# Sliding-window attention with sinks and a token-and-channel mixer: sink outputs and turned u in half-row bursts, finer copies and masks in the first batch

## The chip, the cores and the metric

One Trainium2 chip, one of its cores. The engines run side by side, each in the order of its own instructions: TensorE (PE) multiplies into PSUM, VectorE (DVE), ScalarE (ACT) and GpSimd (POOL) work on tiles, SyncE (SP) issues transfers. Weight loads of TensorE are shown as PEld. The metric is device time in microseconds (us), lower is better; the kernel before takes 214.96 us, the median of 3 runs (214.73 to 215.01).

## The reference

Inputs q, k, v are 4 batches of 8 heads, 768 positions and 64 columns. Each position attends to the last 128 positions and to the first 4 (the sinks). The heads' outputs side by side are x (768 x 512 per batch), which a mixer takes:

```python
keep = (pos[None, :] < 4) | ((rel >= 0) & (rel < 128))
a = softmax(where(keep, q @ k.T / 8, -1e9))
x = heads_side_by_side(a @ v)
u = x + (relu(x.T @ w_tok1) @ w_tok2).T        # 768 -> 256 -> 768 over tokens
out = u + relu(u @ w_ch1) @ w_ch2              # 512 -> 1536 -> 512 over channels
```

## The kernel before, in words

Heads are worked in pairs: 16 pairs, four to a batch, a pair's two heads on the two halves of 128 partitions. Matmuls are in bf16. For a pair, q and k are transposed on TensorE (`transpose_whole` with full rows for pairs 0 to 4, `transpose_halves` with 64 rows for the later ones, line 416) and copied from PSUM into `qT`, `kT` (`prepare`, line 361). `score` (line 422) multiplies them for three groups g of two key tiles, each key tile against its own and the next query tile; as a head has 64 columns, these matmuls use half of the array's rows, one head on each half. In the first batch masks are added by matmuls with `ident` inside the same unit (line 439); later DVE multiplies by them after the exponential (line 472). `score_sinks` (line 493) makes the four sink columns of two pairs at once. `pv` (line 514) multiplies the probabilities with v, whose 65th column of ones gives the row sums, for half of the query tiles and both heads; the sinks' part is one matmul of 128 rows and 130 columns per query tile from the third on. A reciprocal and a product (line 539) write `x_sb`.

Token mixing runs over halves of the 512 columns: `mix_h`, `mix_u`, and u turned for the channels (`transpose_u` with full rows in the first batch, `transpose_u_halves` with half rows later, line 642). `mix_channels` makes 24 units `v1` and then `out_part` per 128 tokens; its matmuls are most of TensorE's work.

A burst here is a run of half-row matmuls between full-row ones. PSUM has two double banks "sc" (scores, transposes of q and k) and four banks "mx" (all the rest).

The order of instructions is set when the kernel is built. Each unit of TensorE is an `Op` with what it waits for, the banks it needs and the copies and exponentials that follow it. `Plan.run` (line 305) goes through assumed costs and gives out the unit that can begin first: those of the first batch by a fixed preference among lists, then channel mixing ("main") and the next batch's attention and token mixing ("side"), with the side finished at 0.6 of the main. DVE, ACT and POOL take the other work by assumed earliest end, and `urgent` breaks ties. So each engine has a fixed order, and what comes later than assumed holds up what stands behind it.

Loads of q and k of the first four pairs go out on SP's queue and are cast to bf16 by ACT and DVE (`cast`, line 867); all other loads go out on POOL's queue and are cast on the way. `keep_warm` (line 137) puts matmuls on a tile of ones into the stream: seven at the start, seven with the first transposes, and two with each score unit of pair 0 (line 453).

Of the kernel before, what the change touches and what calls it, by code (L numbers as in the profile page):

```python
# [16 lines left out]
def kernel(  # L17
# [28 lines left out]
    NQ = 6  # L46

# [12 lines left out]
    given = []  # L60

    def bank(tag, *shape, dtype=FP32, slot=None):

        n = given.pop(0) if slot is None else slot
        return psum.tile([P, *shape], dtype, name=f"ps_{tag}", tag=f"{tag}{n}", bufs=1)
# [154 lines left out]
    class Op:  # L220
        def __init__(self, cost, fn, deps=(), tag=None, then=(), size=0.0, lag=None, loads=0):
            self.cost, self.fn, self.deps, self.tag, self.then = cost, fn, list(deps), tag, list(then)
            self.done = None
            self.lag = SEM if lag is None else lag
            self.size = size
            self.urgent = 0
            self.loads = loads
            self.banks = 1
# [6 lines left out]
    class Plan:  # L235
# [26 lines left out]
        def start_pe(self, op):  # L262
# [3 lines left out]
            if op.tag:  # L266
                free = self.slots(op.tag)
                if len(free) < op.banks:
                    return None
                t = max(t, free[op.banks - 1][0])  # L270
# [24 lines left out]
        def commit_pe(self, op, t):  # L295
            if op.tag:
                given[:] = [n for _, n in self.slots(op.tag)[:op.banks]]
                for n, readers in zip(given, op.readers):
                    self.held[op.tag][n] = readers
# [51 lines left out]
    def unit(ns, fn, deps=(), tag=None, then=(), readers=None):  # L351
        op = Op({"PE": float(ns)}, fn, deps, tag, then, size=float(ns))
# [3 lines left out]
        op.readers = [list(then)] if readers is None else readers if tag == "sc" else [readers]  # L356
# [4 lines left out]
    def prepare(p):  # L361

        kT, ks = kTb[p % NKB], kTs[p % NHP]

        def evict_q(e):
            t = att_pool.tile([P, S], BF16, name="qT2")
            view, ps = tiles["ps_q", p]
            copy(e, view(t), ps)
            tiles["qT", p] = t

        def evict_k(e):
            view, ps = tiles["ps_k", p]
            copy(e, view(kT), ps)
# [8 lines left out]
        cost = {"DVE": 950.0} if 0 < p < NHP else {"DVE": 950.0, "ACT": 900.0}  # L382
        done["qT", p] = Op(cost, evict_q, [("sk", p - 2)] if p >= 2 else [])
        done["kT", p] = Op(dict(cost), evict_k, [("s", p - NKB)] if p >= NKB else [])
        done["qT", p].urgent = done["kT", p].urgent = 2 * (p < NHP)
# [5 lines left out]
    def transpose_whole(p, n):  # L391
# [13 lines left out]
        then = [done[name + "T", p]] + ([done["kTs", p]] if n else [])  # L405
        done["t" + name, p] = unit(340, run, [done[name + "_bf", p]], "mx", then, then)
        return done["t" + name, p]

    def transpose_halves(p):

        ps = bank("sc", 2, 8 * P, dtype=BF16)[:, :, 0:2 * NT * D].rearrange("d x (n j p) -> d x n j p", n=2, j=NT)
        for n in range(2):
            for j in range(NT):
                for x in range(2):
                    rows = ds(D * x, D)
                    in_order(nc.tensor.transpose(ps[:, x, n, j], bfs[p, n][rows, j], ident[rows, rows]))  # L416
            tiles["ps_" + "qk"[n], p] = (
                lambda t: t.rearrange("d (x p j) -> d x p j", x=2, j=NT), ps[:, :, n].rearrange("d x j p -> d x p j"),
            )


    def score(p, groups, nxt=None):


        pe_mask = p < NHP

        def width(g):
            return 3 * P if g == NT // 2 - 1 else 4 * P

        def run():  # L430
            if nxt is not None:
                transpose_halves(nxt)
            if 0 in groups:
                tiles["pT", p] = pt_pool.tile([P, 2, NT, 2, P], BF16, name="pT")
            for g in groups:
                ps = tiles["ps_s", p, g] = bank("sc", 2, 4 * P)
                if pe_mask:
                    for i in range(2):
                        mm(
                            ps[:, i, 0:width(g)], ident,  # L440
                            mask_adds[g == 0].rearrange("p k n q -> p (k n q)")[:, 0:width(g)], start=True, stop=False,
                        )
            for g in groups:
                for k in range(2):
                    kt = 2 * g + k
                    nq = 2 if kt < NT - 1 else 1
                    for i in range(2):
                        mm(
                            tiles["ps_s", p, g][:, i, ds(2 * k * P, nq * P)], tiles["kT", p][ds(D * i, D), ts(kt, P)],
                            tiles["qT", p][ds(D * i, D), kt * P:(kt + nq) * P], start=not pe_mask, stop=True,  # L450
                        )
            if p == 0:
                keep_warm(2, plan.spare())

        def part(t, g):
            return t.rearrange("p i k n q -> p i (k n q)")[:, :, 0:width(g)]

        then, readers = [], []
        if nxt is not None:
            then += [done["qT", nxt], done["kT", nxt], done["kTs", nxt]]  # L460
# [502 lines left out]
```

## Time and profile before

| | |
|---|---|
| Median of 3 runs | 214.96 us (214.73 to 215.01) |
| The profiled execution | 214.58 us, span 212.8 us |
| TensorE busy | 204.9 us, 96% |
| VectorE, ScalarE, GpSimd busy | 54%, 53%, 31% |
| First exponential begins | 8.78 us |
| Last exponential of the first batch ends | 25.24 us |
| First matmul of channel mixing | 34.99 us |
| Last set of u turned | 167.03 us |

Times count from the first instruction. Busy time of TensorE includes pipelining, so one matmul's length is more than what it costs in a stream; the distance from one start to the next tells that. A line of a group names the source line, engine, operation, output and inputs, and how many.

### The profile page before, as it was taken

The page shows a single profiled execution, that of the slowest core. Times are in us where ns is not written, and L with a number is a line of the kernel's source. Part 1 is how long each engine was busy: PE and PEld are TensorE (multiplying, and loading weights), DVE is VectorE, ACT ScalarE, POOL GpSimd, SP SyncE. Part 2 cuts the span into 40 slices and gives each one's busy share as a digit, 9 for nine tenths or more (in the row PEclk, how much of TensorE's full clock was granted, in tenths as well). Part 3 has the DMA queues.
Part 4 walks back from the last instruction along what each step waited for, and adds up shares of the span by engine and source line. Part 5 has one row for each costly group of instructions (what it writes and reads, how often), then busy time and mean ns, then how long its engine had stood idle before and what let it go on. Part 6 is the DMA issues. An engine that isn't in the chain of part 4 may idle for free.

```text
span 212.8 us, 4838 instructions
## 1 busy us (share of the span) xinstructions
PE 204.9 (96%) x2032; PEld 121.2 (57%) x2052; DVE 115.5 (54%) x233; ACT 112.6 (53%) x211; POOL 65.8 (31%) x84
## 2 busy tenths in 40 slices
PE   6999999999999999999999999999999999999994
PEld 2436686556665654565765644656666445655443
DVE  4688564757769452877676445586783522000222
ACT  3678575779748112897774150797772102774000
POOL 6297659794699980054000000000000000000000
PEclk9999999999999999999999999999999999999999
DMA  6999999999999999039501112100000123000222
GB/s 197 256 261 182 172 174 190 148 150 194 160 151 141 200 184 203 21 22 93 39 0 52 51 52 99 49 3 2 3 0 3 75 108 112 4 0 0 102 99 99
DMA packets 73221, 21.55 MB, mean 101 GB/s; under 512 B 63216, under 2 KB 70256, under 8 KB 73200
## 3 DMA queue, kind: packets, MB, share of 16 engines
q0 software_dynamic: 67232, 11.80, 71.3%
q1 hardware_dynamic: 5968, 9.45, 12.7%
q8 instruction: 16, 0.26, 0.5%
q14 instruction: 5, 0.04, 0.1%
HBM read 26.75 MB, written 6.29 MB: 155 GB/s over the span
## 4 chain that ended last, share of the span: by engine, by line
PE 80%; ACT 10%; DVE 5%; issue 3%; DMA 1%; DVEq 0%
PE ps_mx L108 69%; PE ps_sc L108 7%; ACT pT L464 3%; ACT qT L115 2%; PE ps_mx L111 2%; ACT v1T L121 2%; DVE kT L117 2%; DMA q_f<-in_q_dram 1%; PE ps_sc L416 1%; DVE x_sb L539 1%; PE ps_mx L653 1%; DVE u_sb L631 1%; ACT kTs L115 1%; DVE recip L536 1%; ACT v_sink L115 0%
## 5 line engine op out<-in xcount | busy, mean ns | idle before, releaser
L108 PE MATMUL ps_mx<-uT,w_ch 128*128 128x384 bf16 x384 | 68.2, 326 | 0.7
L108 PE MATMUL ps_mx<-w_ch,v1T 128*128 128x512 bf16 (+2 forms) x300 | 63.9, 362 | 1.1 <-issue 0.3
L108 PEld LDWEIGHTS <-w_ch 128*128 128x128 bf16 x384 | 35.7, 98 | 25.9 <-DVE x_sb L539 2.3
L121 ACT ACTIVATE v1T<-ps_mx 128x384 bf16<-128x384 f32 x67 | 32.1, 493 | 28.1 <-PE ps_mx L108 16.7
L464 ACT ACTIVATE pT<-ps_sc 128x1024 bf16<-128x1024 f32 (+1 forms) x48 | 44.1, 952 | 3.8 <-PE ps_sc L108 3.3
L108 PEld LDWEIGHTS <-v1T 128*128 128x128 bf16 x312 | 29.0, 98 | 29.9 <-issue 0.7
L778 DVE TENSOR_TENSOR o_sb<-ps_mx,u_sb 128x512 f32<-128x512 f32 x23 | 15.9, 691 | 47.7 <-PE ps_mx L108 45.8
L101 POOL DMA_DIRECT2D v_aug<-in_v_dram x16 | 16.4, 1026 | 16.9 <-ACT qT L115 15.8
L108 PEld LDWEIGHTS <-w_tok 128*128 128x128 bf16 x192 | 18.4, 98 | 5.1 <-issue 1.3
L93 POOL DMA_DIRECT2D q_bf<-in_q_dram x24 | 19.6, 822 | 4.8 <-DMA w_ch<-in_moe_w_ch_dram 2.3
L93 POOL DMA_DIRECT2D k_bf<-in_k_dram x24 | 19.8, 830 | 3.8 <-DVE x_sb L539 1.7
L631 DVE TENSOR_TENSOR u_sb<-ps_mx,x_sb 128x512 bf16<-128x512 f32 x22 | 14.1, 685 | 7.3 <-PE ps_mx L108 7.3
L472 DVE TENSOR_TENSOR pT<-pT,mask_main 128x1024 bf16<-128x1024 bf16 (+1 forms) x24 | 14.6, 619 | 6.2 <-ACT pT L464 6.2
L117 DVE COPY kT<-ps_sc 128x768 bf16<-128x768 bf16 x11 | 10.5, 957 | 13.0 <-ACT qT L115 13.0
L108 PEld LDWEIGHTS <-pT 128*128 128x128 bf16 x352 | 15.8, 98 | 2.9 <-issue 1.7
L123 DVE TENSOR_SCALAR v1T<-ps_mx 128x384 bf16<-128x384 f32 x29 | 15.6, 550 | 3.0 <-PE ps_mx L108 2.8
L108 PE MATMUL ps_mx<-v_aug,pT 128*128 128x65 bf16 x352 | 17.2, 194 | 0.0
L539 DVE TENSOR_TENSOR x_sb<-ps_mx,recip 128x384 bf16<-128x384 f32 x32 | 16.9, 550 | 0.3
L108 PE MATMUL ps_sc<-qT,kT 64*128 64x256 bf16 x192 | 15.8, 263 | 0.4
L115 ACT ACTIVATE uT<-ps_mx 128x768 bf16<-128x768 bf16 (+1 forms) x9 | 6.7, 745 | 13.4 <-PE ps_mx L653 13.2
L108 PE MATMUL ps_mx<-h1T,w_tok 128*128 128x256 bf16 x96 | 12.4, 273 | 0.2
L108 PE MATMUL ps_mx<-v_sink,pT_sink 128*128 128x130 bf16 x64 | 12.2, 219 | 0.0
(63 smaller groups left out, 160.0 us busy)
## 6 DMA issues: line engine op xcount, KB each, us to landing
out_dram<-o_sb SPq DMA_DIRECT2D x23, 256.0 KB, 2.0
v_aug<-in_v_dram POOLq DMA_DIRECT2D x16, 192.0 KB, 7.1
w_ch<-in_moe_w_ch_dram POOLq DMA_DIRECT2D x8, 384.0 KB, 9.2
q_bf<-in_q_dram POOLq DMA_DIRECT2D x24, 96.0 KB, 7.2
k_bf<-in_k_dram POOLq DMA_DIRECT2D x24, 96.0 KB, 6.6
q_f<-in_q_dram SPq DMA_DIRECT2D x4, 384.0 KB, 5.9
k_f<-in_k_dram SPq DMA_DIRECT2D x4, 384.0 KB, 6.3
w_tok<-in_moe_w_tok_dram POOLq DMA_DIRECT2D x2, 384.0 KB, 9.3
```

The lines of the kernel that those rows point to most:

```text
L93: in_order(nc.gpsimd.dma_start(out=out[:, h], in_=rows[:, h]))
L101: in_order(nc.gpsimd.dma_start(out=v_aug.rearrange("p i t d -> p (i t) d")[:, :, 0:D], in_=v[b].rearrange("h s d -> (h s) d")[2 * hp * S:2 ...
L108: in_order(nc.tensor.matmul(*args, skip_group_check=True, **kwargs))
L115: in_order(nc.scalar.activation(out, in_, AF.Copy))
L117: in_order({"DVE": nc.vector, "POOL": nc.gpsimd}[e].tensor_copy(out=out, in_=in_))
L121: in_order(nc.scalar.activation(out, in_, AF.Relu))
L123: in_order(nc.vector.tensor_scalar_max(out=out, in0=in_, scalar1=0.0))
L464: in_order(nc.scalar.activation(part(tiles["pT", p][:, :, ds(2 * g, 2)], g), tiles["ps_s", p, g][:, :, 0:width(g)], AF.Exp, scale=scale,))
L472: in_order(nc.vector.tensor_tensor(out=pt, in0=pt, in1=m, op=ALU.mult))
L539: in_order(nc.vector.tensor_tensor(out=x_sb[b][:, ts(half, QH), ts(hp, 2 * D)].rearrange("p t (i d) -> p t i d", i=2), in0=tiles["ps_o", p ...
L631: in_order(nc.vector.tensor_tensor(out=u_part(b, g, s0, n), in0=tiles["ps_u", b, g, s0], in1=x_sb[b][:, s0:s0 + n, c0:c0 + cn], op=ALU.add,))
L778: in_order(nc.vector.tensor_tensor(out=o_sb.rearrange("p (g c) -> p g c", g=2), in1=u_rows(b, st), in0=tiles["ps_out", b, st].rearrange("p ...
```

## The change

The planner's units may now need banks of both kinds, and a unit can be put together of pieces (`burst`). Scores, transposes of the next pair, the sinks' part of the outputs and turned u become such pieces:

- **Sinks.** For pairs 4 to 14 the sinks' part is made by `sink_values` as eight half-row matmuls of 65 columns, one head on each half of the rows and in its own bank, in the burst of the next pair's first scores; `values` follows per head instead of per half of the query tiles. Pair 15 and the first batch keep `pv`.
- **Turned u.** Five of six sets go into a burst with scores, one of them in an "sc" bank; the last stays alone.
- **First batch.** q and k of pairs 0 to 3 are copied from PSUM in two halves, by ACT or DVE, and the first scores of a pair wait only for the first halves. Masks are units of their own which need nothing but a bank. The two matmuls on ones after each score unit of pair 0 are gone. The second half's token units are preferred to the first's. GpSimd casts q and k of pair 3. Assumed landing times and `urgent` values differ.
- **Order.** The second half's token mixing of a batch stands after the first burst of the next batch, and `score_sinks` of two pairs before the second burst of the first of them.

```diff
+    def burst(*pieces):
+
+        need = {}
+        for p in pieces:
+            for tag, banks in p.need.items():
+                need.setdefault(tag, []).extend(banks)
+
+        def run():
+            for p in pieces:
+                p.fn()
+
+        op = unit(
+            190 + sum(p.size for p in pieces), run, [d for p in pieces for d in p.deps], need,
+            [t for p in pieces for t in p.then],
+        )
+        for p in pieces:
+            for key in p.keys:
+                done[key] = op
+        return op
...
+        parts = 2 if p < NHP else 1
...
+            view, ps = tiles["ps_" + name, p]
+            to = view(t)
+            if parts == 2:
+                ps, to = ps[:, ts(part, P // 2)], to[:, ts(part, P // 2)]
+            copy(e, to, ps)
...
-        cost = {"DVE": 950.0} if 0 < p < NHP else {"DVE": 950.0, "ACT": 900.0}
-        done["qT", p] = Op(cost, evict_q, [("sk", p - 2)] if p >= 2 else [])
+        free = ([("sk", p - 2)] if p >= 2 else [], [("s", p - NKB)] if p >= NKB else [])
+        if parts == 2:
+            cost = {"DVE": 540.0, "ACT": 500.0}
+        else:
+            cost = {"DVE": 950.0} if p < NHP else {"DVE": 950.0, "ACT": 900.0}
+        for n, name in enumerate(("qT", "kT")):
+            done[name, p] = [
+                Op(dict(cost), lambda e, n=n, part=part: evict(e, n, part), free[n]) for part in range(parts)
+            ]
+            for part, op in enumerate(done[name, p]):
+                op.urgent = (3 - part if parts == 2 else 0)
...
+    def transposed(p):
+
+        def run():
+            ps = bank("sc", 2, 8 * P, dtype=BF16)[:, :, 0:2 * NT * D].rearrange("d x (n j p) -> d x n j p", n=2, j=NT)
+            for n in range(2):
+                for j in range(NT):
+                    for x in range(2):
+                        rows = ds(D * x, D)
+                        in_order(nc.tensor.transpose(ps[:, x, n, j], bfs[p, n][rows, j], ident[rows, rows]))
+                tiles["ps_" + "qk"[n], p] = (
+                    lambda t: t.rearrange("d (x p j) -> d x p j", x=2, j=NT), ps[:, :, n].rearrange("d x j p -> d x p j"),
+                )
...
+    def masked(p, g):
+
+        def run():
+            ps = tiles["ps_s", p, g] = bank("sc", 2, 4 * P)
+            for i in range(2):
+                mm(
+                    ps[:, i, 0:width(g)], ident,
+                    mask_adds[g == 0].rearrange("p k n q -> p (k n q)")[:, 0:width(g)], start=True, stop=False,
+                )
+
+        x = done["exp", p, g] = Op({}, None)
+        done["mask", p, g] = unit(width(g) * 0.84, run, [], {"sc": [[x]]})
+        return done["mask", p, g]
+
+    def scores(p, g):
+
+
+        by_pe = ("mask", p, g) in done
+
+        def run():
+            if ("pT", p) not in tiles:
...
-            if p == 0:
-                keep_warm(2, plan.spare())
...
+            if not by_pe:
+                tiles["ps_s", p, g] = bank("sc", 2, 4 * P)
...
+        deps = [*done["qT", p], *done["kT", p]] if g else [done["qT", p][0], done["kT", p][0]]
+        deps += [done["mask", p, g]] if by_pe else []
+        return piece(width(g) * 0.47, run, deps, {} if by_pe else {"sc": [[x]]}, then, [("s", p)])
...
+        def run():
+            for i in range(2):
+                tiles["ps_o", p, i] = bank("mx", NT, D1)
+            for qt in range(2, NT):
+                for i in range(2):
+                    rows = ds(D * i, D)
+                    mm(
+                        tiles["ps_o", p, i][:, qt], tiles["pT_sink", p][rows, ts(qt - 2, P)], vsk[rows, i],
+                        start=(qt == 2), stop=False,
+                    )
...
+            def norm(e, i=i):
+                in_order(nc.vector.tensor_tensor(
+                    out=x_sb[b][:, :, ds((2 * hp + i) * D, D)], in0=tiles["ps_o", p, i][:, :, 0:D],
+                    in1=tiles["recip", p, i].to_broadcast([P, NT, D]), op=ALU.mult,
+                ))
...
+        return piece(
+            120, run, [done["p", p, NT], done["vs", p]], {"mx": [[done[n, p, i] for n in "rx"] for i in range(2)]}, [],
+        )
+
+    def values(p, i):
+
+        def run():
+            pT, v_aug = tiles["pT", p], vs[p]
+            for qt in range(NT):
+                out = tiles["ps_o", p, i][:, qt]
+                mm(out, pT[:, i, qt, 0], v_aug[:, i, qt], start=False, stop=(qt == 0))
+                if qt >= 1:
+                    mm(out, pT[:, i, qt - 1, 1], v_aug[:, i, qt - 1], start=False, stop=True)
+
...
-            ps = tiles["ps_uh", b, g] = [bank("mx", nct, NT, D, dtype=BF16) for _ in range(2)]
+            if tag == "sc":
+                both = bank("sc", 2, 8 * P, dtype=BF16)[:, :, 0:nct * NT * D]
+                both = both.rearrange("c x (k t p) -> c x k t p", k=nct, t=NT)
+                ps = [both[:, x] for x in range(2)]
+            else:
+                ps = [bank("mx", nct, NT, D, dtype=BF16) for _ in range(2)]
...
+        need = {"sc": [ops]} if tag == "sc" else {"mx": [[o] for o in ops]}
+        return piece(350, run, [done["u", b, g, s0] for s0 in range(0, NT, 2)], need, ops)
...
+            prepare(p)
+        turned = [transpose_whole(p, n) for p in range(NHP) for n in range(2)]
+        masks, scored, out = [], [], []
+        for p in range(NHP):
+            for g in range(NT // 2):
+                if p < MASKED_BY_PE:
+                    masks.append(masked(p, g))
+                if g == 0 or p < MASKED_BY_PE:
+                    scored.append(burst(scores(p, g)))
+                elif g == 1:
+                    scored.append(burst(scores(p, 1), scores(p, 2)))
+                if g == 0 and p == NHP - 1:
+                    scored.append(score_sinks(p))
+            if p == 1:
+                out.append(score_sinks(p))
+            if p % 2:
+                out += [pv(n, half) for n in (p - 1, p) for half in range(2)]
+        tokens = []
+        for g in range(2):
+            tokens.append([mix_h(0, g, t, 1) for t in range(NTOK)] if g else [mix_h(0, g, 0, NTOK)])
+            tokens[g] += [mix_u(0, g, st, 2, st == 2) for st in range(0, NT, 2)]
+            tokens[g] += [transpose_u(0, g, st, 2) for st in range(0, NT, 2)]
+        return scored, masks, turned, out, *tokens[::-1]
...
+        units += [transpose_whole(first, n) for n in range(2)]
+        for p in range(first, last + 1):
+            b, hp = pairs[p]
+            pieces = []
+            if p < last:
+                prepare(p + 1)
+                pieces.append(transposed(p + 1))
+            pieces.append(scores(p, 0))
+            if p > first:
+                pieces.append(sink_values(p - 1))
+            if p == last:
+                pieces.append(turned_u(b, 0, "sc"))
+            units.append(burst(*pieces))
+            if p > first:
+                units += [values(p - 1, i) for i in range(2)]
+            pieces = [scores(p, 1), scores(p, 2)]
+            if hp == 0 and p > first:
+                units.append(mix_h(b - 1, 1, 0, NTOK))
+                units += [mix_u(b - 1, 1, st, 2) for st in range(0, NT, 2)]
+                pieces.append(turned_u(b - 1, 1))
+            if hp == NHP - 1 and p < last:
+                pieces.append(turned_u(b, 0))
+            if hp % 2 == 0:
+                units.append(score_sinks(p + 1))
+            units.append(burst(*pieces))
+            units[-1].then.append(sink_rows(p))
+            if hp == 2:
+                units.append(mix_h(b, 0, 0, NTOK))
+                units += [mix_u(b, 0, st, 2) for st in range(0, NT, 2)]
+            if hp == 0 and p > first:
+                parts.append(units)
                 units = []
...
-        cost = {"DVE": 570.0} if p or n else {"ACT": 850.0}
+        cost = {"POOL": 850.0} if p == NHP - 1 else {"DVE": 570.0} if p or n else {"ACT": 850.0}
...
-    for p, at in enumerate(((3950.0, 5000.0), (7000.0, 8050.0), (9900.0, 11300.0), (12600.0, 13700.0))):
+    for p, at in enumerate(((3900.0, 5300.0), (7500.0, 8600.0), (11300.0, 12500.0), (13500.0, 14700.0))):
```

272 lines of the change are left out of this document (107 added, 165 removed).

## The prediction

> **What bounds the kernel now.** I read the page first, then the sums by stage, then the chain of waits, and last the order of time of TensorE around one pair. From the page:
>
> ```profile
> span 212.8 us, 4838 instructions
> PE 204.9 (96%) x2032; PEld 121.2 (57%) x2052; DVE 115.5 (54%) x233; ACT 112.6 (53%) x211; POOL 65.8 (31%) x84
> PEclk9999999999999999999999999999999999999999
> DMA  6999999999999999039501112100000123000222
> ```
>
> TensorE is busy 96% of the span at an undisturbed clock; nothing else passes 57%. So time comes out only where TensorE's own stream gets shorter or where it stands still. DMA is full until about 85 us, so loads land at fixed times, and an earlier TensorE may run into them. The sums by stage (columns: busy us of each engine, clock, DMA share, GB/s):
>
> ```profile
> 8.35:24.00 15.65, 15.08 (x168) 7.47 (x171) 11.48 (x20) 11.62 (x19) 11.30 (x14) 1.00 1.89 222
> 24.00:35.00 11.00, 10.44 (x141) 8.84 (x142) 6.94 (x15) 6.62 (x13) 8.79 (x11) 1.00 1.79 183
> 35.00:62.00 27.00, 26.64 (x291) 16.08 (x290) 17.85 (x35) 19.86 (x40) 20.64 (x26) 1.00 1.89 163
> ```
>
> 8.35 to 24 is the attention of the first batch, 24 to 35 its token mixing, from 35 on batches overlap. Even in the first batch TensorE is nearly full, but not all of that is needed work. The chain of waits there (start, length, what):
>
> ```profile
> 8.74 0.55 PE ps_mx L108 x2
> 9.29 0.04 issue
> 9.33 0.83 PE ps_mx L111 x12
> 10.16 0.76 PE ps_sc L108 x6
> 10.92 0.16 issue
> 11.08 0.38 PE ps_mx L108
> 11.46 0.60 PE ps_sc L108 x6
> 12.06 0.55 PE ps_mx L108 x2
> ```
>
> The pieces at 8.74, 11.08 and 12.06 are matmuls on "ones" that only keep TensorE busy, and they lie on the path. One pair later, TensorE in order of time:
>
> ```profile
> 44.70 0.35 PE L416 MATMUL ps_sc<-ident,q_bf 64*128 64x64 bf16 x12
> 44.88 0.34 PE L416 MATMUL ps_sc<-ident,k_bf 64*128 64x64 bf16 x12
> 45.06 0.38 PE L108 MATMUL ps_sc<-qT,kT 64*128 64x256 bf16 x4
> 45.37 0.36 PE L108 MATMUL ps_mx<-v_aug,pT 128*128 128x65 bf16 x6
> 45.57 0.22 PE L108 MATMUL ps_mx<-v_sink,pT_sink 128*128 128x130 bf16 x1
> 45.63 0.29 PE L108 MATMUL ps_mx<-v_aug,pT 128*128 128x65 bf16 x4
> ```
>
> Read the starts, since lengths overlap: 24 half-row transposes take 45.06 - 44.70 = 0.36 us, 0.015 each; a sink matmul of 130 columns holds the stream for 0.06; four of 65 columns hold it for about 0.12, 0.03 each.
>
> **The change, part by part.** *Sinks inside the burst.* Eleven pairs (5th to 15th) change. One now takes 45.37 to 46.29 = 0.92 us: 22 matmuls of 65 columns and 4 of 130. The 22 stay (22 x 0.03 = 0.66). The four sink matmuls, 4 x 0.06 = 0.24, become eight of half rows and 65 columns, two heads side by side in two banks. The nearest row is the transposes (half rows, 64 columns, also in two banks): 8 x 0.015 = 0.12. The burst is entered and left anyway. 0.92 becomes about 0.78: 11 x 0.14 = -1.5 us, all on TensorE and so on the path. Ends: nothing gained if the halves do not overlap (8 x 0.03 = 0.24), -2.6 if they were free. I take -1.5, because the transposes have the same tiles and weights. The two normalisations per pair stay 550 ns each on DVE.
>
> The Trainium skill (TensorE: Matmul & The Clock Gate, "Wait — 56ns, not 53.3ns?") speaks against this: starts never come closer than about 25 ns, however few columns. By that floor eight would take 0.20 and the eleven pairs would give 0.4 us. The transposes' rows, 24 in 0.36 us, do not keep to it, and the measurement decides.
>
> *Transposed u inside bursts.* Of six sets, three already follow half-row scores directly (66.1, 110, 123 us), and the last (167.0) stays alone. Two gain. At 77.93 the matmul before the set starts at 77.62 (77.19 and two of 0.22) and the one behind it at 78.62; less 0.22 for the former, the set holds the stream for 0.78 us, against 24 x 0.015 = 0.36 inside a burst, 0.42, of which 0.16 is idle behind it. At 156.46 the isolated set takes 0.55 (to 156.91, with the switch in front), 0.2 more than inside. Together -0.6, -0.4 if that idle time returns; I take -0.5.
>
> *Matmuls on ones.* Six go, at 0.22 each: -1.3, on the path as the chain shows. Zero if TensorE then waits for the same things.
>
> *Copies of q and k by halves, scores that need only the first half, masks as units.* ACT takes 810 ns for 768 columns and 600 for 512, so a half is about 0.50 and two cost 0.18 more than one; DVE goes from 957 to two of about 0.55, 0.15 more. That is +1.3 us of engine time over eight copies, while DVE loses two casts of 0.6. In 8.35 to 24 both engines have about 4 us free, which hides it; without this cover half of it, 0.65, would be paid. The first scores of a pair come about 0.5 us earlier, and q and k need not follow each other on DVE. What is late on the path now is the stalls of 0.16 (10.92) and 0.15 twice (17.60, 21.61): -0.5, zero if others replace them. A mask now runs when its bank is free, behind no copy. The first two go ahead of the first transposes, at a time when 512 columns still take 0.43 us (seven on ones in 3.17 us) rather than 0.22: 4 x 0.43 = 1.7 us from 4.4 on, delaying those transposes from 4.8 to 6.1. But k's were held by ones until 6.62, and one of the two masks ran behind them anyway: I put +0.3, ends 0 and +0.9.
>
> *Casts of pair 3 on GpSimd.* Its one cast, 520 columns, took 642 ns: 768 make 0.95, two 1.9. Queued behind them on POOL's queue are a load of w_tok and then those of pair 4 (issued at 14.45, landed 24.2 to 26.2), behind w_tok, which lands at 23.56. That backlog of 9 us hides it. If it didn't, pair 4's k would land at 28.1, before its use at 29.14. SP's queue is untouched.
>
> *Order after the attention.* From the last exponential's end (25.24) to the first channel matmul (34.99) pass 9.75 us with some 8.95 of TensorE work; the second half's tokens now go first and the first half's fill. -0.5 of the 0.8 that is waiting; ends 0 and -0.8.
>
> *New waits.* A burst is one unit in order: now it waits for its sink exponential, two "mx" banks and u too, and everything behind it on TensorE waits along. Sixteen bursts get such a condition. The nearest rows are idle times of 0.15 in front of two bursts (106.5, 152.6) and none before the rest: 2 x 0.15 = +0.3; ends 0 and 16 x 0.25 = +4.0 (half of a relu of 0.49 that holds a bank).
>
> Sum: -1.5 - 0.5 - 1.3 - 0.5 + 0.3 - 0.5 + 0.3 = -3.7 us. The profiled execution took 214.58 (span 212.8 and 1.8 around it), so it would be 210.9; it lies 0.4 under the median of 214.96, which makes the forecast **211.3**. Best ends together: -2.6 - 0.6 - 1.3 - 0.5 - 0.8 = -5.8, 209.2.
>
> **Rivals.** *The first batch gains nothing.* ACT becomes its bound: exponentials 8 x 1.02 + 4 x 0.81 = 11.4, two sink ones 1.2, eight small copies 1.3, eight halves 4.0: 17.9 us from 5.6 on ends at 23.5 at best, against 25.24 now, and any wait eats that. For it: ACT's only long waits there are for scores (3.3 us), of which half copies placed ahead of exponentials would use most. Against: TensorE, at 15.08 of 15.65, is fuller. Then 214.96 - 1.5 - 0.5 + 0.3 = 213.3.
>
> *Halves that issue one by one.* The sinks give nothing: 212.8. The transposes' rows speak against it. (This is the rule above, which would leave 0.4 of it: 212.4.)
>
> *A fuller gain.* The tail loses all its waiting, no burst waits, and the masks in front cost nothing: 211.3 - 0.9 = 210.4, and with sinks nearer to free 209.5.
>
> *Slower: bursts that wait.* If the two "mx" banks a burst needs are freed only by a relu that began late, TensorE stands in front of each of the sixteen. At 0.35 us each that is 5.6 instead of 0.3: 216.6. It decides from (3.7 + 0.3) / 16 = 0.25 each. For it: short stalls on these banks are there (0.13 at 47.9, 55.0, 100.1 and 146.2, behind DVE's x_sb). Against: none is longer, and work of the channel mixing is there to be put between.
>
> *No change*, a mixture of the smaller failures, 215.0. Loads cap only more than is forecast: pair 5 lands at 33.88 and is used at 36.39, pair 6 at 41.59 and 44.70; a first batch earlier by 1.7 to 2 us stays within 2.5.
>
> **How the numbers follow.** Forecast 0.54; first batch without gain 0.15; halves one by one 0.05; fuller gain 0.09; slower 0.12; no change 0.05. Faster by over 0.2% (0.43 us, about what a measurement of this kernel tells from none): the first four, 0.83; same 0.05; slower 0.12. The range from 209.4 to 214.2 holds the forecast with its terms' nearer ends and the first three rivals, about 0.8, and leaves out the slower one, no change and the best ends together.
>
> **What would show it.** Right: the 22 matmuls of a pair in about 0.66 us, eight of sinks in 0.12 inside the burst; two bursts fewer after 35 us; fourteen matmuls on ones instead of twenty; the first channel matmul near 33 us instead of 34.99; the 35 to 168 stretch shorter by about 1.7. Wrong: starts of the sink halves 0.03 apart; idle time in front of bursts, released by DVE or ACT; TensorE between 8 and 22 us waiting for ACT; first transposes beyond 6.2 us that carry through to the first exponential (8.78 now); pair 5's transposes waiting for their load.

## The result, and the profile after

The changed kernel takes 211.84 us (median, 211.41 to 212.16), beside 214.84 us (214.58 to 215.01) for the kernel before on the same chip: a ratio of 0.986, 95% interval 0.9836 to 0.9885. The forecast was 211.3, so the total is right within 0.6 us (3.0 us gained, where 3.7 were forecast). Its parts are not, as the stages show. The profiled execution took 211.41 us. From the page of the changed kernel:

```profile
span 209.6 us, 4916 instructions
PE 200.8 (96%) x2071; PEld 122.2 (58%) x2090; DVE 114.7 (55%) x250; ACT 112.6 (54%) x200; POOL 67.4 (32%) x86
```

TensorE is still busy 96% of a shorter span: its stream got shorter, and it stands still about as much as before. The sums by stage of the changed kernel (columns as in the prediction: window, length, busy us of TensorE, weight loads, DVE, ACT, POOL, then clock, DMA share, GB/s):

```profile
8.35:22.00 13.65, 12.85 (x155) 7.35 (x158) 10.12 (x26) 12.05 (x20) 12.53 (x15) 1.00 1.70 226
22.00:33.00 11.00, 10.88 (x150) 9.53 (x149) 6.67 (x15) 7.31 (x13) 6.97 (x10) 1.00 1.96 175
...
35.00:62.00 27.00, 26.46 (x295) 16.28 (x296) 17.12 (x36) 19.39 (x35) 20.96 (x26) 1.00 1.90 164
```

The tail of the first batch (second line) now has TensorE busy 10.88 of 11.00, where 10.44 of 11.00 stood before. But from 35 to 62 us it is busy 26.46 of 27 instead of 26.64: more standing still than before, in a stage where the bursts are.

First exponentials begin between 8.1 and 9.7 us in the profiled executions of all kernels here (8.83 in this one, 8.78 before). I therefore split each span at two marks and count from mark to mark:

| | first exponential to first channel matmul | first channel matmul to end |
|---|---|---|
| before | 26.21 | 177.81 |
| after | 23.37 | 177.44 |
| gained | 2.84 | 0.37 |
| forecast | 2.0 | 1.7 |

How well these two stages repeat can be read from the kernels further down. Where the order of TensorE's work behind the first channel matmul is the same, the second stage agrees within 0.01 us (177.44 and 177.44 for the changed kernel and "ones back", 177.37 and 177.38 for "whole copies" and "pair 3 cast by DVE"). The first stage scatters more: seven kernels with the same order in it (the changed one, the two with sinks as before, "kTs on DVE" and the three edits of the changed kernel with copies on ACT) take 23.36 to 24.04 us. So in single profiles a few tenths count in the second stage, and not in the first.

The chain of waits of the changed kernel in the first batch:

```profile
8.83 1.03 ACT pT L506
9.87 0.04 issue
9.91 0.48 PE ps_sc L109 x2
10.39 0.34 PE ps_mx L112 x6
10.73 0.59 PE ps_sc L109 x5
```

The matmuls on ones that stood at 8.74, 11.08 and 12.06 are gone; a mask (9.91, in "ps_sc") and transposes follow the exponential directly, and TensorE stands 0.46 us for it, in front of that mask. TensorE in order of time around the same pair as before:

```profile
...
44.04 0.34 PE L456 MATMUL ps_sc<-ident,k_bf 64*128 64x64 bf16 x12
44.21 0.38 PE L109 MATMUL ps_sc<-qT,kT 64*128 64x256 bf16 x4
44.43 0.29 PE L109 MATMUL ps_mx<-v_sink,pT_sink 64*128 64x65 bf16 x8
44.65 0.84 PE L109 MATMUL ps_mx<-v_aug,pT 128*128 128x65 bf16 x22
45.33 1.46 PE L109 MATMUL ps_mx<-uT,w_ch 128*128 128x384 bf16 x8
47.23 0.65 PE L109 MATMUL ps_mx<-uT,w_ch 128*128 128x384 bf16 x3 [0.43 <-ACT v1T L122]
```

From the start of the scores to the first channel matmul: 45.06 to 46.29, 1.23 us, before; 44.21 to 45.33, 1.12 us, now. The stream of a pair did get 0.11 us shorter. The last line shows what came for it: 1.9 us after the outputs TensorE stands for 0.43 us, waiting for a relu on ACT, where it stood for 0.13 before, for DVE's `x_sb`. This happens four times (47.23, 92.98, 104.64, 141.43).

### The profile page after: what moved, and what is told of

The parts are those of the page before. It is cut to its first block, busy times and chain, and to the rows that moved or that the text cites. A ratio compares the mean times of both kernels' runs of the same rounds, so it can differ in the third digit from the quotient of the medians.

```text
span 209.6 us, 4916 instructions
## 1 busy us (share of the span) xinstructions
PE 200.8 (96%) x2071; PEld 122.2 (58%) x2090; DVE 114.7 (55%) x250; ACT 112.6 (54%) x200; POOL 67.4 (32%) x86
## 4 chain that ended last, share of the span: by engine, by line
PE 90%; ACT 5%; DVE 3%; issue 1%; ACTq 0%
PE ps_mx L109 77%; PE ps_sc L109 8%; PE ps_mx L112 2%; DVE kT L118 2%; PE ps_sc L456 2%; ACT qT L116 2%; ACT v1T L122 1%; ACT pT L506 1%; PE ps_mx L742 1%; ACT kTs L116 1%; DVE u_sb L713 0%; DVE ones L136 0%; PE ps_sc L742 0%; DVE o_sb L920 0%; ACTq L116 0%
## 5 line engine op out<-in xcount | busy, mean ns | idle before, releaser
L109 PE MATMUL ps_mx<-uT,w_ch 128*128 128x384 bf16 x384 | 67.4, 326 | 1.0 <-ACT v1T L122 0.9
L122 ACT ACTIVATE v1T<-ps_mx 128x384 bf16<-128x384 f32 x73 | 35.8, 492 | 30.4 <-PE ps_mx L109 20.1
L109 PEld LDWEIGHTS <-w_ch 128*128 128x128 bf16 x384 | 36.2, 98 | 24.8 <-issue 2.0
L118 DVE COPY kT<-ps_sc 128x768 bf16<-128x768 bf16 x11 | 10.5, 958 | 13.1 <-ACT qT L116 13.1
L124 DVE TENSOR_SCALAR v1T<-ps_mx 128x384 bf16<-128x384 f32 x23 | 12.8, 555 | 6.7 <-PE ps_mx L109 6.5
L109 PE MATMUL ps_mx<-v_aug,pT 128*128 128x65 bf16 x352 | 14.9, 194 | 0.0
L109 PEld LDWEIGHTS <-pT 128*128 128x128 bf16 x352 | 13.3, 97 | 1.7 <-DVE recip L569 0.2
L116 ACT ACTIVATE qT<-ps_sc 128x768 bf16<-128x768 bf16 x11 | 8.9, 810 | 9.8 <-PE ps_sc L456 9.7
L109 PE MATMUL ps_mx<-x_sb,w_tok 128*128 128x256 bf16 x96 | 11.8, 273 | 0.0
L612 DVE TENSOR_TENSOR x_sb<-ps_mx,recip 128x384 bf16<-128x384 f32 x22 | 11.5, 552 | 0.1
```

Of the source, the lines that this page charges most:

```text
L109: in_order(nc.tensor.matmul(*args, skip_group_check=True, **kwargs))
L116: in_order(nc.scalar.activation(out, in_, AF.Copy))
L118: in_order({"DVE": nc.vector, "POOL": nc.gpsimd}[e].tensor_copy(out=out, in_=in_))
L122: in_order(nc.scalar.activation(out, in_, AF.Relu))
L124: in_order(nc.vector.tensor_scalar_max(out=out, in0=in_, scalar1=0.0))
L612: in_order(nc.vector.tensor_tensor(out=x_sb[b][:, :, ds((2 * hp + i) * D, D)], in0=tiles["ps_o", p, i][:, :, 0:D], in1=tiles["recip", p, i ...
```

## The experiments

All are edits of the changed kernel unless said otherwise. Medians in us, ratio to the kernel before, and the two stages of the profiled execution. The runs were made in groups on different chips, each with the kernel before beside it (214.84 with the changed kernel, then 214.57, 214.49 and 214.70), so kernels of different groups are better compared by their ratios (0.01 is 2.1 us). The ratios are taken over all runs of a kernel and differ a little from those of the medians:

| kernel | median | ratio, 95% interval | exp. to channel | channel to end |
|---|---|---|---|---|
| after | 211.84 | 0.986 (0.9836 to 0.9885) | 23.37 | 177.44 |
| sinks as before | 211.32 | 0.9841 (0.9813 to 0.9869) | 23.36 | 176.60 |
| sinks and u as before | 211.50 | 0.9875 (0.9843 to 0.9906) | 23.73 | 177.40 |
| ones back | 212.61 | 0.9912 (0.9885 to 0.9938) | 24.35 | 177.44 |
| whole copies | 212.47 | 0.9904 (0.9876 to 0.9932) | 23.78 | 177.37 |
| masks with scores | 213.64 | 0.9968 (0.995 to 0.9986) | 25.60 | 177.70 |
| pair 3 cast by DVE | 211.90 | 0.9873 (0.9849 to 0.9897) | 24.04 | 177.38 |
| these four together | 213.25 | 0.9949 (0.993 to 0.9969) | 26.72 | 176.34 |
| kTs on DVE | 211.47 | 0.9865 (0.9845 to 0.9886) | 23.72 | 177.39 |
| copies on ACT | 209.04 | 0.9749 (0.9728 to 0.977) | 23.58 | 175.07 |
| copies on ACT, sinks as before | 209.62 | 0.9776 (0.9744 to 0.9807) | 24.04 | 175.33 |
| copies on ACT, side to 0.55 | 209.90 | 0.9775 (0.9754 to 0.9797) | 23.36 | 175.05 |
| kernel before, copies on ACT | 212.02 | 0.988 (0.9859 to 0.9901) | 26.36 | 175.79 |

### Where did the 1.7 us after 33 us go?

**Sinks as before.**

```diff
-            if p > first:
-                pieces.append(sink_values(p - 1))
...
-                units += [values(p - 1, i) for i in range(2)]
+                units += [pv(p - 1, half) for half in range(2)]
```

> All of the change but the sinks: pairs 4 to 14 take them again by four full-row matmuls of 130 columns inside the outputs. The kernel with the whole change took 211.8. Theory A (the sinks save 0.13 us a pair on TensorE, but in four places TensorE, now earlier, stands 0.43 us for a bank that a relu on ACT holds, where it stood 0.13 before): those four waits go back to about 0.13, and the time is 211.8 + 1.4 - 1.2 = 212.0. Theory B (the four waits come from bursts that hold banks, not from TensorE being earlier): they shrink by less, yet the whole 1.4 is lost: 213.2. Theory C (the halves do not overlap): the outputs of a pair take the stream no longer than before, and the time is 211.8 or less.

Measured 211.32, not slower than the whole change, and under all that was expected if the sinks saved time (212.0 and 213.2). TensorE around the pair in this kernel (last piece of the outputs, then channel matmuls):

```profile
45.72 0.28 PE L109 MATMUL ps_mx<-v_aug,pT 128*128 128x65 bf16 x4
45.85 2.41 PE L109 MATMUL ps_mx<-uT,w_ch 128*128 128x384 bf16 x12
```

The outputs again take 0.92 us (44.93 to 45.85), so the halves do overlap, and twelve channel matmuls run without the 0.43 us wait (the list of TensorE's idle times has 0.13 us there, as in the kernel before, four times). The wait of 0.60 and 0.17 us at the border between the first two batches, shown further down, is not there either. The second stage is 0.84 us shorter (176.60 beside 177.44): the sinks' new form shortens the stream of each pair, and brings waits that cost more.

**Sinks and u as before.** Each `turned_u(...)` becomes a unit of its own besides (one of three places shown):

```diff
...
-                pieces.append(turned_u(b - 1, 1))
+                units.append(burst(turned_u(b - 1, 1)))
...
```

> Sinks by full rows as in the run above and each of the six sets of turned u as a unit of its own: only the first batch and the order of the token mixing remain of the change. If u in bursts is worth the 0.5 us forecast, 0.5 above the run without sinks, 212.5 by theory A and 213.7 by B; if sets fall next to scores anyway, no difference from it. The first channel matmul stays at 32.2 us.

Measured 211.50. The totals do not part it from the last one (intervals 0.9813 to 0.9869 and 0.9843 to 0.9906), but the second stage does: 177.40 against 176.60, 0.8 us longer. TensorE changes between half and full rows 58 times behind the first channel matmul in this kernel and 50 times in the last one, and such a change costs about 0.095 us (worked out below): 8 x 0.095 = 0.76. That is what u gains in bursts. The kernel before has 54 changes, the changed kernel 48.

**What the 0.43 us wait for.** All engines of the changed kernel from 44.4 us on (in brackets: idle time in front, and what released it):

```profile
44.48 0.81 ACT L116 ACTIVATE qT<-ps_sc 128x768 bf16<-128x768 bf16 x1
45.32 0.96 DVE L118 COPY kT<-ps_sc 128x768 bf16<-128x768 bf16 x1 [2.11 <-ACT qT L116]
46.31 0.35 ACT L116 ACTIVATE kTs<-ps_sc 64x4 bf16<-64x4 bf16 x2 [1.02 <-DVE kT L118]
46.69 0.49 ACT L122 ACTIVATE v1T<-ps_mx 128x384 bf16<-128x384 f32 x1
```

The copies of q and k were meant to run side by side on ACT and DVE. They run one behind the other: DVE begins k at 45.32, 0.03 us after ACT ends q at 45.29, having stood still for 2.11 us. ACT then stands 1.02 us for k, copies the sink columns, and only at 46.69 begins the relu (`v1T`) that frees the "mx" bank TensorE waits for; it ends at 47.18, and TensorE goes on at 47.23. This is in both kernels. Over the span, from the waits of the changed kernel (total us, times, longest):

```profile
DVE kT L118 <- ACT qT L116: 13.1, 10, 2.3
ACT kTs L116 <- DVE kT L118: 8.2, 8, 1.0
```

In the built program DVE's copy of k carries a wait on ACT's semaphore: q and k of a late pair lie in the same two banks of PSUM. The Trainium skill (PSUM — Partial Sum Buffer, "PSUM bank collisions raise a hardware error") says that the compiler back end's scheduler adds a dependency between any two instructions on different engines that touch one bank and the same 32 partitions, two reads included. The trace agrees: 0.03 us from the one's end to the other's start, for all eleven pairs whose copies leave these banks, in both kernels. No run here shows what the chip would do without the wait.

**kTs on DVE.** If ACT's wait for k is the trouble, take it off ACT.

```diff
-            {"ACT": 440.0, "DVE": 400.0}, sink_columns, [("sk", p - NHP)] if p >= NHP else [],
+            {"ACT": 440.0, "DVE": 400.0} if p < NHP else {"DVE": 400.0}, sink_columns, [("sk", p - NHP)] if p >= NHP else [],
```

> The whole change, with the small copies of the sink columns (kTs) of pairs 4 to 15 on VectorE alone, so that ACT's relu is not queued behind them. After the change ACT stands 1.02 us for VectorE's copy of kT before kTs, and the relu that frees the bank begins 0.46 us late. If this queue makes the four waits of 0.43: they shrink to about 0.1 and the time from 211.8 to 210.4. If the banks of the normalisation bind instead (VectorE now gets to them 0.33 later): the waits stay, named by x_sb, 211.8 or more.

Measured 211.47, no gain that can be told from none. TensorE's list of this kernel:

```profile
46.06 1.46 PE L109 MATMUL ps_mx<-uT,w_ch 128*128 128x384 bf16 x8
47.76 1.47 PE L109 MATMUL ps_mx<-uT,w_ch 128*128 128x384 bf16 x8 [0.24 <-DVE x_sb L612]
```

The wait only changes its releaser: DVE now has the sink columns in front of `x_sb`, whose bank is the next to be needed (0.24, four times). At the border between two batches TensorE waits 1.30 and 0.17 us instead of 0.60 and 0.17.

**Copies on ACT.** One engine for q, k and kTs of pairs 4 to 15, so that nothing is handed over at all.

```diff
         else:
-            cost = {"DVE": 950.0} if p < NHP else {"DVE": 950.0, "ACT": 900.0}
+            cost = {"ACT": 830.0}
...
-            {"ACT": 440.0, "DVE": 400.0}, sink_columns, [("sk", p - NHP)] if p >= NHP else [],
+            {"ACT": 440.0, "DVE": 400.0} if p < NHP else {"ACT": 360.0}, sink_columns, [("sk", p - NHP)] if p >= NHP else [],
```

> The whole change, with both copies of q and k and kTs of pairs 4 to 15 on ACT. In the trace VectorE's copy of kT begins 0.03 us after ACT's of qT ends, every time, so the two engines gain nothing by sharing one pair's copies, while VectorE stands 13 us in all. If this chain (2.15 us from q's copy to kTs) and what is queued behind it on two engines makes the four waits: VectorE is free for reciprocals, products and relus, the waits go, 210.1 to 210.6. If ACT, 54% busy and now with some 9 us more, becomes late itself: exponentials come later, 212.5 or more.

Measured 209.04, ratio 0.9749 (0.9728 to 0.977): the fastest kernel of this study, by the ratios 2.4 us under the changed one (2.8 by the medians, which are of different groups). More than was expected (210.1 to 210.6). All engines of it around the same pair:

```profile
44.00 0.81 ACT L116 ACTIVATE qT<-ps_sc 128x768 bf16<-128x768 bf16 x1
44.71 0.80 ACT L116 ACTIVATE kT<-ps_sc 128x768 bf16<-128x768 bf16 x1
44.86 1.95 PE L109 MATMUL ps_mx<-uT,w_ch 128*128 128x384 bf16 x11
45.40 0.34 ACT L116 ACTIVATE kTs<-ps_sc 64x4 bf16<-64x4 bf16 x2
45.71 0.56 DVE L124 TENSOR_SCALAR v1T<-ps_mx 128x384 bf16<-128x384 f32 x1
```

Both copies are over 1.51 us after the first began, where they took 1.80 (44.48 to 46.28); DVE, which has no copy to stand for, takes the relu at 45.71, and eleven channel matmuls run through. The four waits are gone. The stage from the first channel matmul fell by 2.37 us (177.44 to 175.07), and four waits at their price in the stream make 2.4. That price is more than the 0.43 of the row. A channel matmul takes 0.165 us in an unbroken run, so after eight of them, begun at 45.33, the ninth was due at 46.63; it began at 47.23, 0.60 late. By the same count the 0.13 us waits cost 0.29. The edit changes more than the hand-over: the planner now gives DVE 32 of the 96 relus (`v1T`) instead of 23. How much of the gain is the missing hand-over and how much the new division, no run parts, and both copies on DVE were not tried.

**The same edit on the kernel before.**

```diff
-            cost = {"DVE": 950.0} if 0 < p < NHP else {"DVE": 950.0, "ACT": 900.0}
+            cost = {"DVE": 950.0} if 0 < p < NHP else {"DVE": 950.0, "ACT": 900.0} if p < NHP else {"ACT": 830.0}
...
-            {"ACT": 440.0, "DVE": 400.0}, sink_columns, [("sk", p - NHP)] if p >= NHP else [],
+            {"ACT": 440.0, "DVE": 400.0} if p < NHP else {"ACT": 360.0}, sink_columns, [("sk", p - NHP)] if p >= NHP else [],
```

> The kernel before, with only the copies of q, k and kTs of pairs 4 to 15 on ACT. In it the waits behind those copies are 0.13 us in four places, 0.5 in all. If the copies on two engines cost only what TensorE waits for them: 214.5 - 0.5 = 214.0. If they also hold up work elsewhere, so that the 2.8 us which they gave to the changed kernel are theirs in any kernel: 211.7.

Measured 212.02: alone it is worth nearly what the whole change is worth (ratio 0.988 beside 0.986). The price by idle time fell (it gave 214.0). The other bound (211.7) is about right, but the waits in the list do not explain all of it: four at 0.29 and one more of 0.30 at 111.6, which costs 0.37, make 1.5, and the second stage fell by 2.02 (177.81 to 175.79). The other 0.5 stays open. Its sums by stage:

```profile
35.00:62.00 27.00, 27.00 (x303) 16.56 (x303) 17.11 (x34) 20.80 (x41) 20.68 (x26) 1.00 1.99 171
```

TensorE is busy all of 27.00 us (26.64 before), and so it is in each of the four stages from 35 to 168.

It also corrects a reading of mine. The kernel before has 2052 weight loads but 2032 recorded matmuls; here all 2052 are recorded, and the idle times of 0.15 "after issue" (in front of the bursts at 106.5 and 152.6, and behind u at 78.6) that I took as nearest rows are not there. They were matmuls missing from the record. So were the three stalls of the first batch (at 11.08, 17.60 and 21.61, 0.15 each): this kernel, which gives TensorE the same order there, shows none of them, and at each the record of before has a weight load without its matmul.

**Sinks as before, with the copies on ACT.** Both edits.

> The faster version with q's, k's and kTs' copies of pairs 4 to 15 on ACT (209.0), with the sinks by full rows again. If the sinks' halves save 0.13 us a pair and only the waits behind the copies ate it: now without those waits it shows, 209.0 + 1.4 = 210.4. If the sinks never saved anything on the path: 209.0 within 0.4.

Measured 209.62 beside 209.04: the intervals overlap, so the sinks' 1.2 us (11 pairs by 0.11) do not show in the total even without the four waits. In the second stage they do in part: 175.07 with the sinks in the burst, 175.33 without, 0.26. The kernel with the sinks in the burst waits where this one does not, at the border between the first and the second batch; TensorE of the changed kernel there, and likewise with the copies on ACT (0.60 and 0.17, at 80.8 and 81.5):

```profile
80.77 0.51 PE L742 MATMUL ps_mx<-ident,u_sb 64*128 64x64 bf16 x24
81.88 0.35 PE L456 MATMUL ps_sc<-ident,q_bf 64*128 64x64 bf16 x12 [0.60 <-ACT pT L506]
82.06 0.35 PE L456 MATMUL ps_sc<-ident,k_bf 64*128 64x64 bf16 x12
82.58 0.40 PE L109 MATMUL ps_sc<-qT,kT 64*128 64x256 bf16 x4 [0.17 <-ACT pT L506]
```

Two bursts follow each other with no channel matmul between, and the second one needs "sc" banks that an exponential still reads. In TensorE's stream these two waits cost about 1.1 us: the first transposes come 1.11 behind the start of u (0.36 where a burst follows u without a wait, at 123 us in the kernel before), the scores 0.36 behind the last transposes (otherwise 0.03). They stand in the changed kernel, "ones back", "kTs on DVE" and two kernels with copies on ACT, and in none with the sinks as before; but four other kernels with the sinks in the burst lack them too.

**Side to 0.55.** The share of the main work at which the planner wants the side work finished, to part these two bursts.

```diff
-            f = m / msize / 0.6
+            f = m / msize / 0.55
```

> The faster version, with the side (the next batch's attention) planned to end at 0.55 instead of 0.6 of the channel mixing. At the border of the first two batches TensorE stands 0.60 and 0.17 us for exponentials, since two bursts follow one another with no channel matmuls left between. If that is for want of main work at the end of a batch: the wait goes, 208.3. If the side, earlier, runs into its loads (done at 85 us) or other waits: 209.0 or more.

Measured 209.90, no gain, and both border waits stand there unchanged. That they go (208.3) was wrong; the time is that of the other case (209.0 or more), though no new wait came. Why the order puts these two bursts together in some kernels and not in others stays open.

### What carries the first batch's gain?

**Ones back.**

```diff
+            if p == 0:
+                keep_warm(2, plan.spare())
```

> The whole change, with the six matmuls on ones after pair 0's scores put back. If they lie on the path: 6 x 0.216 = 1.3 us, 213.1, the first channel matmul at 33.5 instead of 32.2. If they only fill time in which TensorE waits (0.46 at 9.9 us, 0.15 at 11.5): 0.7 or less, 212.3 to 212.5.

Measured 212.61, 0.77 above the changed kernel; the first stage is 0.98 longer. The wait of 0.46 us at 9.91 is not there: ones stand in its place.

**Whole copies.**

```diff
-        parts = 2 if p < NHP else 1
+        parts = 1
...
-            cost = {"DVE": 950.0} if p < NHP else {"DVE": 950.0, "ACT": 900.0}
+            cost = {"DVE": 950.0} if 0 < p < NHP else {"DVE": 950.0, "ACT": 900.0}
...
-                op.urgent = (3 - part if parts == 2 else 0)
+                op.urgent = 2 * (p < NHP)
```

> The whole change, with whole copies of q and k in the first batch (VectorE for pairs 1 to 3). If half copies matter: first scores of a pair 0.5 us later, the first channel matmul at about 33, 212.6. If the halves only cost fixed time, since the trace has the second half wait for the first where they lie on two engines: 211.8 or less.

Measured 212.47; the first stage is 0.41 longer, at 23.78 within the scatter of that stage. The intervals of the two totals overlap as well, so this is at most a small gain.

**Masks with scores.** The mask's matmuls go back into the unit of the scores, and so behind the copies that the scores wait for.

```diff
-                    masks.append(masked(p, g))
-                if g == 0 or p < MASKED_BY_PE:
-                    scored.append(burst(scores(p, g)))
+                    m = masked(p, g)
+                    m.keys = []
+                if g == 0 or p < MASKED_BY_PE:
+                    sc = scores(p, g)
+                    sc.deps.remove(m)
+                    scored.append(burst(m, sc))
```

> The whole change, with each mask inside the unit of its scores again. If masks ahead of copies carry a good part of the first batch's 2.8 us: the first channel matmul 0.8 to 1.3 us later than 32.2, 212.7 to 213.1. If they only change the order in a full stream: 211.8 within 0.3; the two masks in front no longer run at half speed, which would give up to 0.4 back.

Measured 213.64, 1.8 above the changed kernel and almost back at the kernel before. Its first stage is 2.23 longer. The sum of that stage:

```profile
8.65:22.00 13.35, 11.88 (x143) 6.41 (x145) 8.48 (x22) 11.06 (x17) 12.04 (x15) 1.00 1.79 229
```

TensorE stands still for 1.47 us there, against 0.80 of 13.65 in the changed kernel, and has done less: in the changed kernel masks are work that it does while copies run.

**Pair 3 cast by DVE.**

```diff
-                cost = {"POOL": 850.0} if p == NHP - 1 else {"DVE": 570.0} if p or n else {"ACT": 850.0}
+                cost = {"DVE": 570.0} if p or n else {"ACT": 850.0}
```

> The whole change, with pair 3's q and k cast by VectorE. If VectorE's share of the first batch matters: two casts of 0.56 in front of copies, the first channel matmul 0.5 later, 212.3. If they were hidden on either engine: 211.8 within 0.4.

Measured 211.90, the same as the changed kernel; its first stage (24.04) is at the end of the scatter.

**These four together.**

> The first batch as before in four points: ones back, whole copies of q and k, masks in the unit of the scores, pair 3 cast by VectorE; the preference among lists stays as changed. If the first batch carries 2.8 us (35.0 to 32.2 at the first channel matmul): 214.3 to 214.6. If only the ones count: 213.1. If the stages after it give back what the first one gains (loads and the side's share): 212 or less, with the first channel matmul late and the stage after it shorter.

Measured 213.25, between what was expected (214.3 to 214.6 if the first batch carries 2.8 us, 213.1 if only the ones count). The first stage is 3.35 us longer, the second 1.1 shorter. But the mark between them has moved against the work. TensorE in this kernel:

```profile
34.02 0.35 PE L456 MATMUL ps_sc<-ident,q_bf 64*128 64x64 bf16 x12
...
34.93 2.11 PE L109 MATMUL ps_mx<-uT,w_ch 128*128 128x384 bf16 x12
```

The burst with pair 5's transposes and pair 4's first scores (34.02 to 34.70) stands in front of the first channel matmul here and behind it in the changed kernel (34.90 to 35.57). So about 0.7 us of both differences is only work on the other side of the mark, and 2.7 and 0.4 are left. The 2.7 is less than the sum of the first three alone (0.98 + 0.41 + 2.23 = 3.6). This kernel has no border wait, but a fifth wait of 0.43 in its place; so have "whole copies" and "pair 3 cast by DVE", whose second stage is as long as the changed kernel's (177.37 and 177.38). That the first batch's gain is given back at the border is therefore not shown.

## Why the prediction came out as it did

**Sinks inside the burst, -1.5: the size in the stream nearly right, the gain absent.** The 22 matmuls take 0.68 (44.65 to 45.33; forecast 0.66). Eight sink matmuls take 0.22 (44.43 to 44.65) with the burst's leaving in it. That leaving costs 0.095, from the scores' 0.31 (45.06 to 45.37, before) against 0.22 (44.21 to 44.43, now) when nothing is left behind them. So the eight hold TensorE for about 0.12, as the transposes' row said. The floor of about 25 ns between starts (the Trainium skill, TensorE: Matmul & The Clock Gate, "Wait — 56ns, not 53.3ns?") is not kept by these pairs in two banks: it would make it 0.20. Their starts lie 4 and 25 to 31 ns apart in turn, so those on one half of the rows are 29 to 35 ns apart. What I left out is that the work of other engines behind the pair does not move up with TensorE. Counted from the first transposes of the burst, the third group of channel matmuls was due at 2.78 us instead of 2.89, and began at 3.37 instead of 3.18: 0.11 of the longer wait is TensorE coming earlier, and 0.20 is a later release, by a relu on ACT instead of DVE's `x_sb`. Why another engine holds the bank now, no run shows; the sinks' new form also takes both "mx" banks inside the burst and splits the outputs by head. With the sinks undone the time does not rise.

**Turned u, -0.5: about right.** The 0.16 "idle behind it" was a gap in the record, which leaves 0.2 for each of two sets, 0.4. The totals cannot tell that from nothing, but the second stage shows the price: 0.8 us when four sets leave the bursts, 0.2 each.

**Six ones, -1.3: right in kind, 0.8 to 1.0 in size.** Part of the time on ones was waiting that stays (0.46 us at 9.91).

**Copies by halves and masks as units, -0.5: the mis-sized term.** Together they are worth 2 to 2.6 us of the first stage, nearly all by the masks (1.8 in the total), while halves give 0.4 to 0.6 at most, and may give nothing. I had priced the stalls that the chain showed, 0.16 and twice 0.15, which were matmuls missing from the record, and not the copies that a mask no longer stands behind. A mask in its own unit is work that can be done at any time a bank is free; without it TensorE stands still 0.7 us more in that stage (1.47 against 0.80) and has less done.

**Masks in front at half speed, +0.3: no cost seen.** Three take 0.41 to 0.43 each from 4.43 us on, the fourth 0.22, and the first transposes begin at 5.91 (forecast 6.1), but the first exponential begins at 8.83, against 8.78: the near end, zero, as far as a time that scatters from 8.1 to 9.7 can tell.

**Order behind the attention, -0.5: about right.** TensorE stands 0.12 instead of 0.56 us in the 11 us of token mixing.

**Casts by GpSimd, 0: right.** The first channel matmul came at 32.20, earlier than the forecast's 33, and no transposes of pair 5 waited for a load.

**New waits, +0.3: the step that failed.** I looked for them in front of the bursts, from two rows that were no waits. They came at the border, and two groups of channel matmuls behind the outputs, at banks whose relu stands on ACT behind a chain of three copies. The rival of waiting bursts had the right kind of bank and the right kind of holder (a late relu on "mx"), and short waits of 0.13 us stood at the same place before, as I had named for it, though behind `x_sb`; but it happened four times, not sixteen. Priced in the stream, the new waits make 4 x 0.60 and 1.1 at the border, 3.5 us; those of before make 1.5 (four at 0.29, one at 0.37). That is 2 us more, under the 4 from which that rival decides. Against it stand the sinks' 1.2 and six changes between half and full rows fewer (48 for 54), 0.6. These would leave the second stage about 0.2 us longer; it is 0.37 shorter, so about half a microsecond is not accounted for. That the sinks' new form brings the longer waits is shown by undoing it; that its shorter stream alone does, or that the border wait is its work too, is not.

So the total was right by luck, because two errors cancelled: about 0.8 us too little in the first batch, and 1.3 too much behind it. Of the other rivals, a first batch without gain fell (2.84 gained), and so did halves that issue one by one (0.12 us for eight, not 0.24).

## What to carry to other kernels

A shorter piece on the busiest engine can be worth nothing if the next thing that it waits for is set by another engine: before pricing it, follow the releaser of the next wait behind the piece one or two steps back, even when that wait is only 0.13 us now. When two engines empty the same bank, look in the trace whether they really overlap; if the one starts where the other ends, try one engine for both (here ACT): it can be faster, and it frees the other. Before a mark between two stages is trusted, look whether the same work lies in front of it, and how far kernels with the same order differ. Work that waits for nothing (masks here) should not stand in one unit with work that does.

## What the runs showed of the hardware

- Copies of q and k out of the same two banks by ACT and DVE never overlapped: for all eleven pairs DVE began 0.03 us after ACT's end (10 times it had stood idle until then, 13.1 us in all). On ACT alone the same pair of copies took 1.51 instead of 1.80 us, and both kernels gained (2.4 us and 2.6 us by their ratios).
- A wait of TensorE costs more in its stream than the idle time that the profile shows for it: 0.13 us of idle time delayed the next matmul by 0.29, 0.43 by 0.60.
- Half-row matmuls of 65 columns on both halves of the rows, in two banks, hold TensorE for about 0.015 us each, and the change between half and full rows costs about 0.095 us (from the start of four score matmuls to what follows, 0.31 with the change and 0.22 without; eight changes more made a stage 0.8 us longer).
- A TensorE idle time of about 0.15 us can be a matmul missing from the record: in the kernel before 20 of 2052 were missing. The profile may even name a releaser for it (17.60 and 21.61 us, DVE).
